# Two scans' loop: which work is given out beside them, and what is queued behind their steps

## The chip, the cores and the metric

One core of a Trainium2 chip runs the whole program. The metric is the time of one execution in microseconds (us), as the device measures it; of the kernel before there are three such times. TensorE (PE) multiplies matrices, VectorE (DVE) and ScalarE (ACT) and GpSimd (POOL) work element by element, and SyncE (SP) issues most of the transfers. Each engine works off its own queue in the order in which the program was laid out.

## The reference

Three layers follow each other. The first is a recurrence over 768 steps for 4 batches with 8 heads of width 40, with a 40 x 40 state for each:

```python
for t in range(S):
    y[:, :, t] = np.einsum('bhd,bhde->bhe', rt, state)
    Sa = np.einsum('bhde,bhe->bhd', state, at)
    state_decay = state * wt[:, :, None, :] - np.einsum('bhd,bhe->bhde', Sa, bt)
    state = state_decay + np.einsum('bhd,bhe->bhde', vt, kt)
# y becomes x: 3072 tokens x 320
h = x @ w_in;  g = np.maximum(h, 0) + alpha * np.minimum(h, 0);  x = g @ w_out      # 320 -> 2048 -> 320
g = x @ w_gate;  out = (g / (1 + np.exp(-g)) * (x @ w_val)) @ w_out                  # 320 -> 1536 -> 320
```

All is float32; the products are made of split operands (a rounded part and its rest), three matmuls for one.

## The kernel before

**Stages.** The 768 steps are cut into 6 blocks m of 128 steps; with 4 batches that makes 24 items, numbered 0 to 23, four for each block. An item goes through `preps` (lines 555 to 638 and 842: decays, scaled operands, small products; all four engines). The four items of one block then share one `inverse(m)` (line 647), the forward substitution that inverts small triangular matrices: VectorE transposes (L650), 31 steps of a product (L665) and a subtraction (L673) on VectorE, each needing the one before, two more transposes (L676, L678), and a tail of tiny matmuls and copies (L686 to L713). Then each item goes through `seq` (line 722), the scan: two chunks of 64 steps, each a strict chain zp (L769), zs (L771, ACT), pp (L779), ut and pv (L781, L783, ACT), transposes (L787, L791), gs and s0 (L793, L798, ACT), gp (L802), a masked product (L805, DVE), yp (L817, L821), the state and the output (L825, L746, L829, DVE and POOL). Two items are scanned side by side. The item's result leaves by a transfer that ScalarE's queue issues (L837). `mlp1(j)` is the first MLP for the tokens of block j, and the second MLP comes last, after all scans.

**Weights.** The inputs' weights are taken apart and rounded into split tiles. For the first MLP, `conv1` makes 32 tiles (two for each of 16 slices f) with two ACT operations (L191, L192), one DVE operation (L193), an ACT copy and a POOL subtraction (L217, L218), and stores them (L264). Twelve of them are made before the first scans. `mlp1` fetches them again (L284).

**The order.** `drive` (line 141) takes several generators with a weight each. At every turn it lets the one that is least far along, by steps done over weight, trace its next step. What is traced earlier gets the higher priority, and a third number lifts a generator's priority; a scheduler then lays each engine's queue out by these priorities and by its own estimate of when operands are ready. The scans and `rest1` have the same lift (`SP` and `HP2`, 3000), the weights' tiles less (`CP`, 2000), `mlp1` none. `rest1` is the chain of what is left of the preparation of items 4 to 7 and `inverse(1)`: 21 steps (one was taken earlier) and 40 steps.

**Ties.** `drive` can also keep the last instruction that each of the first `lead` generators, the scans, has traced on each engine; with `engs` (a bit for each of PE, DVE, ACT, POOL), `lag` and `who`, the other generators' instructions of the same engine must then come behind it in that engine's queue:

```python
if e[4] >= lead and who >> (e[4] - lead) & 1:
    for b in range(4):
        log = crit.get(b, [])
        if engs >> b & 1 and len(log) >= lag:
            st.enter_context(tc.issue_after(log[-lag]))
```

With `engs=0`, the default, nothing is tied. A tie is an order in one queue; it adds no semaphore. Besides, `behind` (line 869) has each tile's DVE instruction come after the last traced step of the substitution.

**Around the change.** Lines 900 to 903 run `inverse(0)` and form `rest1`. Lines 912 to 916 are the loop of scans 0 and 1, here *loop one*; all of `rest1` and 20 tiles go with it. Line 917 gives back the boot pools (two PSUM pools, and buffers of items 0 to 7). Lines 927 to 931 are the loop of scans 2 and 3, *loop two*: nothing of `rest1` is left for it, and 17 steps of `mlp1(0)` go with it. These treat the first 8 slices f for the tokens of batches 0 and 1 alone (256 columns: *half slices*), so that they need only scans 0 and 1; the half slices of batches 2 and 3 and then 8 whole slices follow. `mlp1` has one PSUM buffer for its upper products (line 921). Scans 4 to 7 need `inverse(1)`.

Of the kernel before, what the change touches and what calls it, by code (L numbers as in the profile page):

```python
# [16 lines left out]
FAC = 1.0  # L17
# [28 lines left out]
RA = 1.0  # L46
MP = 0
YB = 1
CP = 2000
HP2 = 3000  # L50
# [23 lines left out]
def kernel(  # L74
# [66 lines left out]
    def drive(*gens, lead=0, engs=0, lag=1, who=0):  # L141
        live = [[*g, 0, j] for j, g in enumerate(gens)]
        names = ["PE", "DVE", "Activation", "Pool"]
        while live:
            e = min(live, key=lambda e: e[3] / e[1])
            try:
                tc.cur_priority -= e[2]
                with ExitStack() as st:
# [5 lines that stand above are left out]
                    n0 = len(traced())  # L154
                    ok = next(e[0], 0)
                    if e[4] < lead:
                        new = traced()[n0:]
                        for b in range(4):
                            mine = [x for x in new if str(x.engine).split(".")[-1] == names[b]]
                            if mine:  # L160
                                crit.setdefault(b, []).append(mine[-1])
                tc.cur_priority += e[2]
                e[3] += 1
                if ok == 0:
                    live.remove(e)
            except StopIteration:
                tc.cur_priority += e[2]
                live.remove(e)

    def chain(*gens):  # L170
        for g in gens:
            yield from g
# [172 lines left out]
    def conv1():  # L345
        for f in range(K1):
            conv(stage, 2 * f, moe_w_in, f, "up")
            yield
            conv(stage, 2 * f + 1, moe_w_out, f, "down")
            yield  # L350

    def conv2():
        for f in range(KEEP):
            for j, (src, kind) in enumerate(((moe2_w_gate, "up"), (moe2_w_val, "up"), (moe2_w_out, "down2"))):
                conv(stage, 2 * K1 + 3 * f + j, src, f, kind)
                yield
# [502 lines left out]
    c1, c2 = conv1(), conv2()  # L859
    NC1, NC2 = 2 * K1, 3 * K2  # L860

    def after(ins, g):
        while True:
            with tc.issue_after(ins.ins):
                if next(g, 0) == 0:
                    return
            yield

    def behind(g):
        while True:  # L870
            with tc.issue_after(mark["inv"].ins) if "inv" in mark else nullcontext():
                if next(g, 0) == 0:
                    return
            yield
# [10 lines left out]
    def take(g, n):  # L885
        for _ in range(n):
            if next(g, 0) == 0:
                return
            yield

    EC0 = 2
    EC = 10
# [5 lines left out]
    c1 = after(mark["prep"], c1)  # L898
    p1, c1 = behind(p1), behind(c1)
    drive((inverse(0), N_INV, HP), (take(p1, EP), EP + .1, BP), (take(c1, EC), EC + .1, CP), lead=1, engs=G0, lag=LG0, who=W0)  # L900
    p1, c1 = after(mark["inv"], p1), after(mark["inv"], c1)
    rest1 = chain(p1, inverse(1))
    nrest = B * N_PREP - EP + N_INV
    if FA == 0:
        drive(
            *((chain(seq(j, j), seq(j + 2, j)), 2 * N_SEQ, SP) for j in range(2)),
            (rest1, FAC * nrest, HP2),
            (take(c1, NC1), NC1 - EC - EC0, CP),
            lead=2, engs=G1, lag=LG1, who=W1,
        )  # L910
    else:
        drive(
            (seq(0, 0), N_SEQ, SP), (seq(1, 1), N_SEQ, SP),
            (take(rest1, int(nrest * RA)) if RA < 1 else rest1, FAC * nrest, HP2),
            (take(c1, NC1), NC1 - EC - EC0, CP),
        )
    boot.close()
    ps1 = ctx.enter_context(ExitStack())
# [7 lines left out]
    if FA:  # L926
        drive(
            (seq(2, 0), N_SEQ, SP), (seq(3, 1), N_SEQ, SP),
            (rest1, FAC * nrest * (1 - RA) + .1, HP2),
            (take(gms[0], 2 * FA + 1), 2 * FA + 1, MP),  # L930
        )
    for m in range(1, NM):
# [201 lines left out]
```

## Time and profile before

| | |
|---|---|
| three runs | 1223.40, 1226.69, 1228.44 us; median 1226.69 us |
| the profiled execution | 1225.27 us, of which its span is 1223.6 us |
| granted TensorE clock, mean of the span | 0.952 |
| PE, DVE, ACT, POOL busy | 1107.1, 735.3, 607.1, 272.0 us |
| loop one's scans (items 0 and 1) | last step 137.3 to 137.7 us |
| `inverse(1)` on VectorE | 120.8 to 185.6 us |
| loop two's scans (items 2 and 3) | last step 178.3 to 178.7 us |

Times in the rows are from the span's start. In a row of the timeline stand the start, the time, the engine (a q behind it: its sequencer, which issues a transfer), the line, the operation, what is written and read, the count, and in brackets the engine's idle time before it with what ended it. A row of the groups gives a line's instructions: count, busy time, mean of one in ns, and idle time before them. A row of the stretches gives its length and then for each engine the busy time and the count, the granted TensorE clock (1.00 is 2.4 GHz), the busy share of the DMA engines and their GB/s.

### The profile page before, as it was taken

What the parts mean: (1) busy time and instruction counts of PE and PEld (TensorE: products, weight loads), DVE (VectorE), ACT (ScalarE), POOL (GpSimd) and SP (SyncE); (2) the same over time, 40 slices, a digit from 0 to 9 for tenths busy, and PEclk for the clock granted to TensorE, in tenths of its full rate; (3) what the DMA queues carried; (4) which work ended last, traced back from release to release, by engine and by line L of the source; (5) the groups of instructions that cost most, each with busy time, mean ns of one, the idle gap of its engine ahead of it and who ended that gap; (6) DMA issues with size and microseconds to landing.
All of it is one profiled execution on the core that took longest, in us unless ns stands there. A gap on an engine that the chain in (4) does not pass through costs nothing. (4 is left out here: it accounts for less than half of the span.)

```text
span 1223.6 us, 24425 instructions
## 1 busy us (share of the span) xinstructions
PE 1107.1 (90%) x9098; PEld 935.2 (76%) x9098; DVE 735.3 (60%) x1592; ACT 607.1 (50%) x1514; POOL 272.0 (22%) x434
## 2 busy tenths in 40 slices
PE   4566678999999989899898999999999999999998
PEld 3345567877878778787686777788788888888887
DVE  7787897698499569859664434879532323223222
ACT  5769658645844764673654433555332323222222
POOL 8115333301212221521363000536300000000000
PEclk9659787999999999899989999999999999999999
DMA  4565697466454544545585473795010101010000
GB/s 145 179 198 176 210 310 228 138 200 185 132 170 137 170 140 148 181 133 147 160 269 189 129 221 135 261 351 158 1 48 1 48 1 48 2 39 9 22 1 21
DMA packets 94884, 166.35 MB, mean 136 GB/s; under 512 B 13232, under 2 KB 43184, under 8 KB 94768
## 3 DMA queue, kind: packets, MB, share of 16 engines
q1 hardware_dynamic: 86608, 160.88, 41.8%
q10 hardware_dynamic: 8160, 3.93, 1.1%
q8 instruction: 72, 1.18, 0.4%
q14 instruction: 44, 0.36, 0.1%
HBM read 136.98 MB, written 27.79 MB: 135 GB/s over the span
## 5 line engine op out<-in xcount | busy, mean ns | idle before, releaser
L217 ACT CAST gh<-g 128x512 fp32r<-128x512 f32 (+1 forms) x176 | 105.5, 600 | 165.0 <-DVE g L1070 115.9
L218 DVE TENSOR_TENSOR gl<-g,gh 128x512 fp32r<-128x512 f32 (+1 forms) x176 | 124.2, 706 | 89.5 <-ACT gh L217 87.1
L1070 DVE TENSOR_TENSOR g<-pv,sg 128x512 f32<-128x512 f32 x72 | 49.8, 691 | 206.3 <-PE pv L294 201.6
L294 PE MATMUL u<-xh,wt 128*128 128x512 f32 (+1 forms) x416 | 147.4, 397 | 11.9 <-DVE g L335 11.0
L335 DVE SCALAR_TENSOR_TENSOR g<-g,neg,u 128x512 f32<-128x512 f32 (+1 forms) x104 | 72.8, 702 | 70.4 <-ACT g L334 69.8
L294 PEld LDWEIGHTS u<-xh,wt 128*128 128x128 f32 x416 | 79.7, 194 | 31.4 <-DVE g L335 14.3
L1068 ACT ACTIVATE sg<-pg 128x512 f32<-128x512 f32 x72 | 43.1, 598 | 121.1 <-PE pg L294 121.1
L294 PE MATMUL pg<-xh,w 128*128 128x512 f32 x288 | 102.5, 394 | 0.0
L294 PE MATMUL pv<-xh,w 128*128 128x512 f32 x288 | 100.4, 389 | 0.0
L334 ACT ACTIVATE g<-u 128x512 f32<-128x512 f32 (+1 forms) x104 | 58.6, 564 | 82.7 <-PE u L294 69.9
L1054 PE MATMUL o<-w,gh 128*128 128x320 f32 x288 | 87.5, 309 | 2.6 <-ACT gh L217 2.6
L1055 PE MATMUL o<-w,gh 128*128 128x320 f32 x288 | 87.8, 309 | 0.0
L301 PE MATMUL d<-gl,wt 128*128 128x512 f32 (+1 forms) x208 | 83.2, 402 | 2.2 <-DVE gl L218 2.2
L604 PE MATMUL mnp<-AN,kbt 128*128 128x128 f32 x384 | 60.1, 307 | 25.6 <-DVE AN L579 13.6
L665 DVE TENSOR_TENSOR tmp<-la 128x96 f32<-128x96 f32 (+43 forms) x306 | 79.5, 286 | 2.7 <-POOL la L653 0.7
L294 PE MATMUL u<-xl,wt 128*128 128x512 f32 (+1 forms) x208 | 80.2, 385 | 0.0
L302 PE MATMUL d<-gh,wt 128*128 128x512 f32 (+1 forms) x208 | 79.9, 386 | 0.0
L1056 PE MATMUL o<-w,gl 128*128 128x320 f32 x288 | 77.2, 310 | 1.0 <-DVE gl L218 0.9
L673 DVE TENSOR_TENSOR la<-la,tmp 128x96 f32<-128x96 f32 (+43 forms) x306 | 76.8, 277 | 2.0
L760 POOL COPY gs<-raw_v 64x160 f32<-64x160 f32 x96 | 43.3, 451 | 148.8 <-PE yp L817 72.2
L618 POOL TENSOR_SCALAR_AFFINE_SELECT AN<-AN 64x256 f32<-64x256 f32 x96 | 50.2, 523 | 117.9 <-ACT AN L617 98.4
L604 PEld LDWEIGHTS mnp<-AN,kbt 128*128 128x128 f32 x384 | 53.4, 214 | 30.0 <-DVE AN L579 13.6
(129 smaller groups left out, 2630.1 us busy)
## 6 DMA issues: line engine op xcount, KB each, us to landing
wt<-wd SPq DMA_DIRECT2D x98, 384.0 KB
wt<-wd SPq DMA_DIRECT2D x98, 320.0 KB
wd<-wc SPq DMA_DIRECT2D x24, 384.0 KB
raw<-in_moe_w_out_dram SPq DMA_DIRECT2D x28, 320.0 KB
raw_bk<-in_bk_dram SPq DMA_DIRECT2D x48, 160.0 KB
wd<-wc SPq DMA_DIRECT2D x20, 320.0 KB
raw<-in_moe_w_in_dram SPq DMA_DIRECT2D x16, 256.0 KB
raw_v<-in_v_dram SPq DMA_DIRECT2D x24, 160.0 KB
```

The costliest lines, as they stand in the source:

```text
L217: nc.scalar.copy(out=h, in_=raw)
L218: eng.tensor_tensor(out=l, in0=raw, in1=h.bitcast(F32), op=ALU.subtract)
L294: last = nc.tensor.matmul(ps, lt, rh, start=(i == 0), stop=(i == len(ops) - 1))
L301: nc.tensor.matmul(ps, wh, gl, start=False, stop=False)
L302: nc.tensor.matmul(ps, wl, gh, start=False, stop=last)
L335: nc.vector.scalar_tensor_tensor(g, g, neg[:, f:f + 1], ps, ALU.mult, ALU.add)
L604: nc.tensor.matmul(ps[:, s].rearrange("p h t -> p (h t)"), kbt[:, g * SH + s].rearrange("p j t -> p (j t)"), an[:, :, g * SH + s, :],)
L665: nc.vector.tensor_tensor(out=tv, in0=ml[:, kk + 1:HALF, kk:kk + 1].to_broadcast([128, nr, ns]), in1=tl[:, kk:kk + 1, c0:c0 + ns].to_broad ...
L673: mark["inv"] = nc.vector.tensor_tensor(out=dst, in0=dst, in1=tv, op=ALU.subtract)
L1054: nc.tensor.matmul(ops[q], gh[:, ts], wh, start=first, stop=False)
L1055: nc.tensor.matmul(ops[q], gh[:, ts], wl, start=False, stop=False)
L1056: nc.tensor.matmul(ops[q], gl[:, ts], wh, start=False, stop=last)
```

## The change

Loop one takes 27 steps of `rest1` and 9 tiles, with weights 27 and 9; since `rest1` has 21 steps of preparation left, the last 6 of the 27 are the first of `inverse(1)` (its first transposition and 5 of the 31 steps). It also ties both: `lead=2` (the two scans), `engs=6` (DVE and ACT), `lag=1` (the newest step), `who=3` (both other generators). Loop two gets the other 34 steps of `rest1`, weight 40, and the other 11 tiles, weight 11, without ties. Nothing is computed in another way.

```diff
     else:
         drive(
             (seq(0, 0), N_SEQ, SP), (seq(1, 1), N_SEQ, SP),
-            (take(rest1, int(nrest * RA)) if RA < 1 else rest1, FAC * nrest, HP2),
-            (take(c1, NC1), NC1 - EC - EC0, CP),
+            (take(rest1, 27), 27, HP2),
+            (take(c1, 9), 9, CP),
+            lead=2, engs=6, lag=1, who=3,
         )
@@
     if FA:
         drive(
             (seq(2, 0), N_SEQ, SP), (seq(3, 1), N_SEQ, SP),
-            (rest1, FAC * nrest * (1 - RA) + .1, HP2),
+            (rest1, nrest - 27, HP2),
+            (take(c1, NC1), NC1 - EC - EC0 - 9, CP),
             (take(gms[0], 2 * FA + 1), 2 * FA + 1, MP),
         )
```

Here `nrest` is 67, `N_SEQ` 13, `NC1` 32, `EC` 10, `EC0` 2, `FA` 8.

## Rows read from the trace of the kernel before

**Rows 1.** The page's busy times of the engines, of the whole span

```profile
PE 1107.1 (90%) x9098; PEld 935.2 (76%) x9098; DVE 735.3 (60%) x1592; ACT 607.1 (50%) x1514; POOL 272.0 (22%) x434
```

**Rows 2.** Stretches: length, then PE, PEld, DVE, ACT, POOL, clock, DMA

```profile
95.00:137.00 42.00, 28.88 (x373) 25.10 (x373) 31.01 (x63) 34.32 (x108) 23.15 (x38) 0.88 0.55 174
137.00:200.00 63.00, 46.38 (x671) 41.27 (x672) 57.36 (x152) 41.51 (x117) 21.66 (x34) 0.77 0.85 278
200.00:700.00 500.00, 467.54 (x5090) 392.18 (x5091) 359.51 (x893) 298.57 (x818) 133.58 (x242) 0.97 0.54 165
...
137.00:183.00 46.00, 34.77 (x376) 30.46 (x376) 43.17 (x132) 27.78 (x87) 16.25 (x27) 0.81 0.86 285
183.00:200.00 17.00, 11.61 (x295) 10.80 (x296) 14.19 (x21) 13.73 (x31) 5.40 (x7) 0.65 0.81 260
...
800.00:1000.00 200.00, 196.38 (x983) 168.74 (x983) 98.47 (x148) 73.29 (x134) 38.26 (x33) 1.00 0.26 85
```

**Rows 3.** ScalarE's groups by line, 95 to 137 us

```profile
L617 ACT COPY AN<-mnp 64x256 f32<-64x256 f32 x12 | 4.4, 367 | 0.2
L610 ACT COPY tt<-mnp 64x256 f32<-64x256 f32 x12 | 4.4, 366 | 0.1
L217 ACT CAST wc<-wz 128x256 fp32r<-128x256 f32 (+2 forms) x12 | 4.3, 391 | 1.6 <-DVE wz L193 0.9 <-DMA wd<-wc 0.7
L191 ACT ACTIVATE wz<-raw 128x384 f32<-128x384 f32 (+1 forms) x8 | 4.2, 528 | 1.2 <-DMA raw<-in_moe_w_out_dram 1.2
L192 ACT ACTIVATE wy<-raw 128x384 uint32<-128x384 uint16 (+1 forms) x7 | 3.7, 528 | 0.0
```

**Rows 4.** Timeline, scans 0 and 1: where ScalarE's copies stand behind TensorE

```profile
95.88 1.15 PE L779 MATMUL pp<-tt,zs 128*64 128x64 f32 x30
...
103.89 0.37 ACT L781 COPY ut<-pp 128x256 f32<-128x256 f32 x1
...
106.83 0.38 PE L791 MATMUL pp<-ident,ST 128*128 128x128 f32 x2
...
110.96 0.61 ACT L793 ACTIVATE gs<-pp 64x160 f32<-64x160 f32 x2
...
119.97 0.98 PE L769 MATMUL zp<-gs,AN 128*64 128x40 f32 x16 [0.77 <-DVE gs L746]
...
122.79 1.18 ACT L771 COPY zs<-zp 64x160 f32<-64x160 f32 x4
...
135.86 0.59 ACT L771 COPY zs<-zp 64x160 f32<-64x160 f32 x2 [3.33 <-PE zp L769]
```

**Rows 5.** VectorE: groups 120 to 138 us, then the substitution's ends (timeline)

```profile
L665 DVE TENSOR_TENSOR tmp<-la 128x31 f32<-128x31 f32 (+11 forms) x12 | 3.8, 348 | 0.3 <-POOL la L653 0.3
L673 DVE TENSOR_TENSOR la<-la,tmp 128x31 f32<-128x31 f32 (+9 forms) x10 | 3.3, 354 | 0.1
...
L650 DVE STREAM_TRANSPOSE la<-tt 128x1024 f32<-128x1024 f32 x1 | 2.0, 1970 | 0.6 <-ACT tt L613 0.6
...
120.79 1.97 DVE L650 STREAM_TRANSPOSE la<-tt 128x1024 f32<-128x1024 f32 x1 [0.62 <-ACT tt L613]
...
183.66 1.91 DVE L678 STREAM_TRANSPOSE tt<-la 128x1024 f32<-128x1024 f32 x1
```

**Rows 6.** Timeline: from the end of scans 0 and 1 to what follows

```profile
137.27 0.41 DVE L829 TENSOR_TENSOR pv<-yp,Wx 128x256 f32<-128x256 f32 x1
...
141.76 0.71 ACT L737 COPY pv<-raw_vt 128x256 f32<-128x256 f32 x2 [3.87 <-DMA raw<-in_moe_w_out_dram]
...
145.18 0.82 SPq L319 DMA_DIRECT2D xa<-xd  x2
...
149.73 0.36 PE L294 MATMUL u<-xh,wt 128*128 128x256 f32 x1
```

**Rows 7.** TensorE's timeline: the first half slices of `mlp1(0)`

```profile
161.62 0.58 PE L294 MATMUL u<-xh,wt 128*128 128x256 f32 x1
...
165.45 0.48 PE L300 MATMUL d<-gh,wt 128*128 128x256 f32 x2
...
167.20 0.40 PE L294 MATMUL u<-xst,wt 128*128 128x256 f32 x2
...
180.53 0.28 PE L294 MATMUL u<-xh,wt 128*128 128x256 f32 x1
```

## The prediction

> **What bounds the kernel now.** I read the busy times of the whole span first. TensorE is busy 1107.1 of 1223.6 us, so 116.5 us are idle in all; VectorE (735.3) and ScalarE (607.1) are far from the span [rows 1]. Next I cut the span into stretches [rows 2]. From 800 us on TensorE is busy 196.4 of 200 us at full clock: that end can't be moved. From 200 to 700 us it is busy 467.5 of 500 us, with VectorE at 72%: TensorE is the limit there too, and work that it has not done by 200 us is simply appended. From 95 to 200 us it is another kernel: 75.3 of 105 us, granted clock 0.88 and then 0.77. There the limit is first ScalarE (34.3 of 42 us up to 137 us) and then VectorE (57.4 of 63 us, and 43.2 of 46 up to 183 us). The change touches nothing outside this stretch, so its value is read there and nowhere else: **how much earlier does TensorE reach the state that it has at 200 us, and how much more has it done by then?** Two numbers carry the answer. L is by how much scans 0 and 1 end earlier than 137 us; S is by how much the substitution's end on VectorE (185.6 us, with the tail that follows it) moves, positive for later.
>
> **Loop one: the ties (L).** ScalarE's timeline shows the cost that they aim at [rows 4]. The pp products of both scans end at 97.0 us, and the first ut copy that reads them starts at 103.9: 6.9 us. The transposes end at 107.2, the gs copies start at 111.0: 3.8 us. The second zp ends at 120.9, the zs copies start at 122.8: 1.8 us. In these 12.5 us ScalarE worked on fillers that had been traced earlier. They were earlier because `rest1` has weight 67: it makes 5.2 steps for each step of a scan, so all 21 steps of preparation are traced by the scans' fifth step of 13. With weight 27 it makes 2.1, and the tie puts each batch behind the newest scan step. So 12.5 us is the upper bound of L. The lower one for a ScalarE that never waits: its 34.3 busy us of this loop, begun at 95 us, end at 129.3 us, which is L = 7.7. If the weights' tiles slip behind the scans (12.2 us of ScalarE's groups, the last three of [rows 3]; they have the lower priority, but 9 of them are still given out here), L grows toward the upper bound. I take **L = 8**, near the lower bound, because the preparation that leaves the first chunk only moves into the second, where ScalarE had room. What the ties can cost below that is the third rival.
>
> What is queued behind the tied instructions: on ScalarE the copies of the preparation (8.8 us in its two largest groups [rows 3]) and the tiles' copies; on VectorE the decays and products of items 5 to 7 and L193; and at the end whatever ScalarE has after the issue of the scans' output transfers (L837), which counts as a step of a scan. Behind those wait GpSimd's selections and subtractions, SP's stores (L264) and the loads that refill the raw buffers. None of these is asked for before the substitution (the copies of item 7) or the later slices (the tiles), so I cost them at nothing as long as the preparation ends with the scans; SP and GpSimd have room (GpSimd 23.2 of 42 us [rows 2]).
>
> **Loop one: the substitution leaves (part of S).** Now it starts at 120.8 us [rows 5], under the second chunk of scans 0 and 1, and has 3.8 + 3.3 + 2.0 = 9.1 us done by 138 us. After the change six steps of it are still traced in loop one, behind nearly all of the scans; I count 3 of the 9.1 us there (the transposition, 2.0 us, and five small steps) and 6.1 us as moved to loop two. The preparation ends some 4 to 8 us later than now, since it is strung along the scans.
>
> **Loop two (S).** VectorE had 43.2 busy us in the 46 us from 137 to 183 [rows 2], a share of 0.94. After the change the same stretch starts L = 8 us earlier, at 129, and holds 6.1 us more: 49.3 / 0.94 = 52.5 us, which ends at 181.5. So **S = -1.5 us**. Within loop two the substitution no longer outranks scans 2 and 3, since both are now traced in turn; that changes who goes first, but both have to be through by the end of this stretch in either kernel (scans 2 and 3 end at 178 us now), so the sum holds. The 11 tiles stay chained to the substitution's steps by `behind`, as now; their VectorE and ScalarE time is in the same stretch before and after, and I cost their move at nothing. If it were not covered, they would be late for the ninth slice, which TensorE reaches only after 16 half slices.
>
> **What TensorE gains.** The scans' result has to reach memory and come back: from the last step at 137.3 us to the new scans' first copy at 141.8, to the load of x at 145.2 and the first upper product at 149.7 [rows 6]. All four hang on scans 0 and 1 and move by L. (The pools that line 917 gives back hang on item 7's preparation; if it ends by 129 us, it is ready long before 145 - 8 = 137.) From there the half slices go one in 4.7 us (161.6 to 180.5 in four) [rows 7], because one PSUM buffer goes round TensorE, ScalarE and VectorE; one of them is 2.15 us of TensorE (165.45 to 167.60). Between their start and the end of the substitution there are now L + S = 8 - 1.5 = 6.5 us more: 6.5 / 4.7 x 2.15 = 3.0 us of work done beforehand. The state of 200 us itself comes 1.5 us earlier. Sum: **1.5 + 3.0 = 4.5 us gained**, and in general gain = -S + (L + S) x 0.46. The tail from 183 to 200 us, where TensorE is busy 11.6 of 17 us at clock 0.65 [rows 2], stays as it is in this sum. What is late next is that tail: the substitution's transposes, tiny matmuls and copies.
>
> The profiled execution took 1225.27 us, 1.4 under the median of the three runs; 1225.3 - 4.5 = 1220.8, and at the median **1226.7 - 4.5 = 1222.2 us**.
>
> **Trace and notes.** The granted clock fell to 0.65 in the tail and was 0.88 in loop one [rows 2]; a mean between the levels of 1.2 and 2.4 GHz (0.5 and 1.0) says that the engine changed between them. If half slices fill idle places there, part of the work would also run at the higher level. I leave that out of the sum and put it into the first rival.
>
> One rule speaks against this change. The Trainium skill, "Perfetto Trace Analysis", section "Optimization Strategy", says that where the most-contended engine changes over time, interleaving the regimes may help. The kernel before does that: VectorE's substitution under ScalarE's preparation. By that rule taking it apart gives the gain back; the second rival prices this from rows, and no row of before tells which wins.
>
> **The rivals.** First, *the whole lead is kept*. L is the full 12.5 us, and VectorE, freed of queues that wait, gets the substitution done as early as the scans: S = -8. Gain 8 + 4.5 x 0.46 = 10.1 us: 1216.6. For it: the idle 30 us of TensorE from 95 to 200 us and the low clock leave the room. Against it: VectorE at 0.94 in the second part [rows 2].
>
> Second, *given back*: L = 8, but the substitution loses its whole cover of 9.1 us, S = +9.1, since it comes second in loop two and its chain of dependent steps finds no other idle place. Gain -9.1 + 17.1 x 0.46 = -1.2 us: 1227.9, no change. The same answer would come if the change did nothing to the order, because the preparation is ScalarE's bound either way.
>
> Third, *the ties make engines wait*, and it is slower. ScalarE works in order; with everything tied behind the newest step, a copy that waits for TensorE holds the fillers up as well. When the scans' copies had no filler before them, they waited up to 3.33 us (135.9 us [rows 4]). There are 8 such stops in two chunks; at some 1.5 us each (my estimate, between nothing and 3.33) that is 12 us, against 7.7 us for which ScalarE is idle in this loop now. Then the scans end 4 us late, L = -4, and the substitution, still without cover, S = 4 + 9.1 = 13.1: gain -13.1 + 9.1 x 0.46 = -8.9 us, 1235.6. It decides from the point where ScalarE's idle time in loop one passes those 7.7 us. For it: TensorE's steps are slow there, at clock 0.88. Against it: each batch of two steps of preparation and most of a tile, some 3 us, is about as long as TensorE's part between two stops.
>
> **How the numbers follow.** The forecast gets 0.45, the whole lead 0.21, given back 0.14, slower 0.20. The forecast's own range is 4 us to either side, 1218.2 to 1226.2. The range for 8 in 10 goes from 1213 (most of the first rival) to 1234 (a part of the third); the rest of the third rival and the far end of the first lie outside. A measurement of this kernel can tell about 0.5%, 6.1 us, from no change: faster means under 1220.6. Of the forecast's 0.45 I put 0.20 below that and 0.25 within; the first rival is all faster; the second all the same; of the third 0.18 are slower and 0.02 the same. Faster 0.41, same 0.41, slower 0.18.
>
> **What would show it.** Right: ut copies within 2 us of the pp products, scans 0 and 1 at their last step at 125 to 132 us, L650 at 124 to 130, the first half slice's product near 141, L678 ending between 180 and 188, and TensorE full from about 195 us, with the later part unchanged. Wrong: ScalarE idle for more than 8 us between 95 and the end of the scans (third rival); L678 past 190 (second); L678 before 180 with the scans at 125 (first). If scans 2 and 3 or the transfers around 130 to 170 us take longer than now, the term of 3.0 us goes. And if anything after 250 us differs by more than a few us, the argument that the rest is only appended is wrong.

## The result, and the profile after

The changed kernel takes 1233.49 us (median of 7 runs, 1229.81 to 1235.4), the kernel before in the same runs 1226.69 (7 runs, 1222.11 to 1229.2): a ratio of 1.0055, 95% interval 1.0037 to 1.0072. It is 6.8 us slower, where 4.5 us faster was forecast; 1222.2 was predicted, and 1233.5 lies at the upper end of the range for 8 in 10 (1213 to 1234). The profiled execution has a span of 1233.5 us at a mean granted clock of 0.944 (before: 1223.6 and 0.952).

The page's busy times of the whole span, which answer to [rows 1]:

```profile
PE 1108.8 (90%) x9098; PEld 941.1 (76%) x9098; DVE 738.9 (60%) x1592; ACT 606.9 (49%) x1514; POOL 268.7 (22%) x434
```

The work is the same. Of the 9.9 us by which the span is longer, TensorE's busy time has 1.7 us and its idle time 8.2. The stretches, as in [rows 2] (length, then PE, PEld, DVE, ACT, POOL, clock, DMA):

```profile
95.00:137.00 42.00, 28.79 (x406) 25.93 (x403) 34.28 (x56) 34.34 (x107) 22.62 (x36) 0.87 0.46 151
137.00:200.00 63.00, 44.42 (x604) 40.22 (x605) 58.25 (x162) 41.52 (x113) 23.08 (x37) 0.72 0.83 268
200.00:700.00 500.00, 462.85 (x5011) 390.63 (x5010) 360.25 (x890) 291.67 (x802) 130.36 (x242) 0.95 0.53 165
137.00:183.00 46.00, 30.52 (x320) 26.87 (x320) 42.75 (x142) 28.61 (x86) 16.54 (x30) 0.79 0.82 267
183.00:200.00 17.00, 13.90 (x284) 13.35 (x285) 15.50 (x21) 12.90 (x28) 6.54 (x7) 0.52 0.85 273
800.00:1000.00 200.00, 196.35 (x974) 167.94 (x973) 102.61 (x153) 74.45 (x137) 43.13 (x38) 1.00 0.29 98
```

Two things are to be seen. From 137 to 183 us TensorE does 4.3 us less than before (30.5 for 34.8), though the scans got there earlier. And from 200 to 700 us, in loops whose code is untouched, it does 4.7 us less (462.9 for 467.5), at a clock of 0.95 for 0.97. Only the end from 800 us on is as it was.

The timeline of the first 200 us, which answers to [rows 4], [rows 5] and [rows 6]: the scans' copies, their last step, the new scans, x, the first half slice, and the substitution's ends.

```profile
94.81 1.15 PE L779 MATMUL pp<-tt,zs 128*64 128x64 f32 x32
95.54 0.37 ACT L781 COPY ut<-pp 128x256 f32<-128x256 f32 x1 [0.81 <-PE pp L779]
...
98.79 0.62 ACT L793 ACTIVATE gs<-pp 64x160 f32<-64x160 f32 x2
...
129.82 0.41 DVE L829 TENSOR_TENSOR pv<-yp,Wx 128x256 f32<-128x256 f32 x1
130.15 1.93 DVE L650 STREAM_TRANSPOSE la<-tt 128x1024 f32<-128x1024 f32 x1
...
134.25 0.71 ACT L737 COPY pv<-raw_vt 128x256 f32<-128x256 f32 x2 [3.46 <-DMA raw<-in_moe_w_in_dram]
...
141.37 0.94 SPq L319 DMA_DIRECT2D xa<-xd  x2
...
154.73 2.03 SPq L284 DMA_DIRECT2D wt<-wd  x4
...
160.30 0.58 PE L294 MATMUL u<-xh,wt 128*128 128x256 f32 x1
...
161.75 0.63 PE L294 MATMUL u<-xst,wt 128*128 128x256 f32 x2
...
184.10 1.93 DVE L678 STREAM_TRANSPOSE tt<-la 128x1024 f32<-128x1024 f32 x1
```

The ut copy now follows its products at once (95.54 for 103.89), the last scan step ends at 130.2 for 137.7, and the substitution begins behind it (130.15) and ends where it did (its last transposition starts at 184.10 for 183.66). But the first upper product of `mlp1(0)` starts at 160.30 instead of 149.73. In the kernel before, 149.73 is only the first of its eight matmuls; the last two, which need the last part of x, come nine us later:

```profile
158.68 0.80 PE L294 MATMUL u<-xst,wt 128*128 128x256 f32 x2
```

Measured by its end the first upper product is late by 2.9 us (162.4 for 159.5): the lead of the scans has turned into a delay on its way.

**A measure for the whole program.** From each trace I took, for every time, how many columns TensorE's matmuls had moved by then. The *lag* of a kernel at a time is how much later it has done what the kernel before had done at that time. For the changed kernel it is -6.1 us at 137 (ahead), +1.1 at 160, +8.9 at 183, +3.6 at 200, +6.1 at 300, +15.7 at 400, +15.0 at 660 and +9.9 from 800 us to the end. The lag rests on one execution of each kernel: two traces of one and the same program (n28 and n28r below) differ by 0.6 us at 200 and by 7.2 at 900. These two executions took 1232.55 and 1225.41 us, and a traced execution isn't always near the median (fetchup's took 1252.8, its median is 1243.5). Where a stop falls on the time asked for, the lag jumps by its length. So only the timed runs decide what a kernel costs, and lags of some us late in the program are no evidence alone.

### The profile page after: what moved, and what is told of

Same layout as the page of the kernel before. It is cut to its first block, busy times and chain, and to the rows that moved or that the text cites. A ratio compares the mean times of both kernels' runs of the same rounds, so it can differ in the third digit from the quotient of the medians.

```text
span 1233.5 us, 24442 instructions
## 1 busy us (share of the span) xinstructions
PE 1108.8 (90%) x9098; PEld 941.1 (76%) x9098; DVE 738.9 (60%) x1592; ACT 606.9 (49%) x1514; POOL 268.7 (22%) x434
## 3 DMA queue, kind: packets, MB, share of 16 engines
q10 hardware_dynamic: 8160, 3.93, 1.1%
## 4 chain that ended last, share of the span: by engine, by line
PE 57%; DVE 16%; DMA 9%; ACT 9%; issue 4%; POOL 2%; SPq 1%; ACTq 0%; DVEq 0%; POOLq 0%
PE pg L294 10%; PE u L294 9%; PE pv L294 9%; PE o L1058 3%; PE o L1057 3%; PE o L1056 3%; PE d L301 2%; PE d L300 2%; PE d L302 2%; PE mnp L604 2%; PE gp L802 2%; DMA xd<-pv 2%; DVE la L673 2%; DVE tmp L665 2%; PE yp L817 2%
## 5 line engine op out<-in xcount | busy, mean ns | idle before, releaser
L218 DVE TENSOR_TENSOR gl<-g,gh 128x512 fp32r<-128x512 f32 (+1 forms) x176 | 122.5, 696 | 89.7 <-ACT gh L217 87.6
L294 PE MATMUL u<-xh,wt 128*128 128x512 f32 (+1 forms) x416 | 147.3, 397 | 7.9 <-DVE g L335 4.5
L294 PE MATMUL pg<-xh,w 128*128 128x512 f32 x288 | 102.5, 394 | 0.0
L294 PEld LDWEIGHTS u<-xh,wt 128*128 128x128 f32 x416 | 79.9, 195 | 27.2 <-DVE g L335 9.3
L294 PE MATMUL pv<-xh,w 128*128 128x512 f32 x288 | 100.5, 389 | 0.0
L294 PE MATMUL u<-xl,wt 128*128 128x512 f32 (+1 forms) x208 | 80.3, 386 | 0.0
L665 DVE TENSOR_TENSOR tmp<-la 128x96 f32<-128x96 f32 (+43 forms) x306 | 76.4, 275 | 2.8 <-POOL la L653 0.9
```

The costliest lines, as they stand in the source:

```text
L218: eng.tensor_tensor(out=l, in0=raw, in1=h.bitcast(F32), op=ALU.subtract)
L294: last = nc.tensor.matmul(ps, lt, rh, start=(i == 0), stop=(i == len(ops) - 1))
L665: nc.vector.tensor_tensor(out=tv, in0=ml[:, kk + 1:HALF, kk:kk + 1].to_broadcast([128, nr, ns]), in1=tl[:, kk:kk + 1, c0:c0 + ns].to_broad ...
```

## The experiments

Ratios are to the kernel before, in runs on the same chip, with the 95% interval; its medians there were 1228.5 to 1230.7 us (1226.7 for the first row). A kernel has 4 to 12 timed runs, the kernel before 7 to 29. The last column counts the TensorE instructions of the loops m = 1 to 5 and of what follows (5768) that stand at another place among themselves than in the kernel before.

| kernel | ratio | lag at 160, 200, 300, 900 us | moved |
|---|---|---|---|
| changed kernel | 1.0055 [1.0037, 1.0072] | 1.1, 3.6, 6.1, 9.9 | 2487 |
| ties | 1.0132 [1.0087, 1.0178] | 9.8, 14.2, 16.0, 19.6 | 3196 |
| shares | 1.0021 [0.9998, 1.0045] | 4.2, 8.1, 5.2, 8.6 | 2835 |
| fetchup | 1.0138 [1.0092, 1.0185] | -3.1, 12.8, 21.1, 27.6 | 3132 |
| fetchlate | 1.0111 [1.0064, 1.0158] | 2.6, 2.6, 12.8, 11.2 | 2858 |
| frz | 1.0084 [1.0061, 1.0107] | 0.7, 3.8, 11.5, 11.1 | 0 |
| rfrz | 1.0051 [1.0028, 1.0074] | 1.0, 0.6, 9.0, 9.8 | 2487 |
| up2 | 1.0087 [1.0061, 1.0112] | 5.8, 7.5, 10.9, 10.7 | 2487 |
| frzup | 1.0099 [1.0060, 1.0138] | 5.4, 8.6, 14.0, 16.6 | 0 |
| frzld | 1.0090 [1.0059, 1.0121] | -0.6, 8.0, 9.4, 11.1 | 0 |
| pv_after | 1.0167 [1.0128, 1.0206] | 3.2, 12.4, 18.1, 27.1 | 2487 |
| pv_before | 1.0180 [1.0145, 1.0216] | 2.6, 2.7, 8.9, 30.3 | 0 |
| n26 | 1.0129 [1.0088, 1.0169] | 0.6, 14.3, 24.0, 26.9 | 2678 |
| n28 | 0.9972 [0.9953, 0.9991] | 3.4, 3.1, 2.3, 7.0 | 2780 |
| n28r, the same again | 0.9970 [0.9949, 0.9990] | 3.9, 3.7, 2.5, -0.2 | 2780 |
| t10 | 0.9971 [0.9950, 0.9992] | 1.0, 10.4, 9.8, 3.7 | 2490 |
| t10r, the same again | 0.9996 [0.9977, 1.0015] | 0.7, 10.5, 9.7, 6.3 | 2490 |
| t11 | 0.9998 [0.9977, 1.0020] | 0.4, -2.2, -3.0, 2.0 | 3086 |
| n28t11 | 1.0025 [1.0009, 1.0041] | 2.9, 7.8, 8.8, 8.9 | 1048 |

### The two halves of the change, and the fetches

*ties* is the kernel before with nothing but the ties; *shares* is the changed kernel without them:

```diff
 # ties: kernel before
             (take(c1, NC1), NC1 - EC - EC0, CP),
+            lead=2, engs=6, lag=1, who=3,
 # shares: changed kernel
             (take(c1, 9), 9, CP),
-            lead=2, engs=6, lag=1, who=3,
```

> The kernel before with the ties of loop one alone; all of rest1 and 20 tiles stay in loop one. Theory A (late fetch: the loss is that the first MLP's first weight fetches stand some 19 us later in SyncE's queue, behind loads and stores of tiles, 154.7 against 135.7 us): decided by where the fetches come to stand, here 5 places later than before, so near the kernel before, within 4 us of 1226. Theory B (lost cover: the substitution no longer runs under the first two scans): here it is given out as before, so no slower than before, 1220 to 1227. Theory C (the ties themselves cost, engines wait in order): slower by about 6, 1231 to 1235.

> The changed kernel without the ties: 27 steps and 9 tiles in loop one, the rest in loop two. Theory A: the fetches stand as late as in the changed kernel, so 1230 to 1236. Theory B: the substitution has lost its cover, 1231 to 1236 as well. Theory C: without the ties no loss, 1224 to 1228. A and B are told apart by the first upper product of the half slices (A: at 158 us or later, with the substitution's end under 186 us; B: the substitution's end past 190 us).

Ties alone cost 1.3%, 15 us, more than any of the theories had (theory C: about 6): scans 0 and 1 end at 149.9 us, 12 later than before, and from 95 us to there ScalarE is idle for 14.8 us (7.7 in the kernel before to its scans' end, 4.2 in the changed one). That is the prediction's third rival by its own sign, ScalarE idle for over 8 us, in the kernel that has the ties without the new weights. The shares alone cost 0.2%, not clear of no change, with the scans' end at 141.6. Together the two cost 0.55%: their effects don't add (1.3 + 0.2), and the scans' lead comes only with both.

*fetchup* gives the first four weight fetches of `mlp1(0)` a higher priority in the changed kernel; *fetchlate* puts those of the kernel before behind its loads of x:

```diff
 # fetchup
-        with held_by(ago(AHEAD)) if idx in resident else nullcontext():
+        with held_by(ago(AHEAD)) if idx in resident else lifted(2500) if j == 0 and len(fetched) < 4 else nullcontext():
 # fetchlate; mark["xa"] is the last load of x (L323)
+        with held_by(ago(AHEAD)) if idx in resident else tc.issue_after(mark["xa"].ins) if j == 0 and len(fetched) < 4 else nullcontext():
```

> The changed kernel with the first four weight fetches of the first MLP lifted by 2500, so that they stand 26 places earlier in SyncE's queue; nothing else is edited. Theory A: the first upper product comes at 142 to 150 us and not at 160.3, and at 200 us TensorE is no longer behind the kernel before; time 1224 to 1229. Theory B and C: the fetch was not what held it, 1231 to 1236.

> The kernel before with the first four weight fetches of the first MLP put behind the loads of x in SyncE's queue (15 places later); nothing else is edited. Theory A: the first upper product moves from 149.7 to about 158 us and the time grows by 3 to 6 us, 1229 to 1233. Theories B and C: within 2 us of before.

fetchup brings the start of the first upper product back to 150.9 us (its end to 158.1), with the scans' lead kept (end at 131.3), and yet the kernel is 1.4% slower than before; of its lag of 27.6 us, 12.8 stand by 200 us already. fetchlate loses 2.6 us by 200 us (3 to 6 were expected in all) and then another 10 between 240 and 300 us, where nothing of the edit is left. So a small edit in the first 160 us changes something far behind it. The orders of the queues say what: the scheduler lays out each queue of the whole program by priorities and by its own estimate of times, and of the 5768 TensorE instructions behind loop two 2487 stand elsewhere in the changed kernel than before (613 of 1182 of ScalarE, 698 of 1238 of VectorE, 241 of 561 transfers of SP), though not a line of theirs was changed. This became theory D: the new order of the untouched loops costs the time.

### Holding the order

To separate the first 200 us from the later order, I wrote an order out in the kernel: the numbers of the instructions traced from loop m = 1 on, engine by engine, as they stand in the other kernel, each tied behind the one before it in its queue (an order only, no semaphore):

```diff
+    for o in ORDER:                       # one list for each engine
+        for p, q in zip(o, o[1:]):
+            tc.add_manual_dep(al[cut + q], al[cut + p].name, NO_SYNC, reason="order")
```

*frz* has the changed first part and the later order of before; *rfrz* has the first part of before and the later order of the changed kernel. Holding costs nothing by itself: with its own later order written out in this way, either kernel is built as the same program as without, instruction for instruction and wait for wait on every engine (12793 in the changed kernel, 12776 in the kernel before).

> The changed kernel, but everything that is traced in the loops m = 1 to 5 and behind them stands on each engine in the order that the kernel before gives it (5768 instructions of TensorE, 1238 of VectorE, 1182 of ScalarE, 300 of GpSimd, 561 transfers of SP); what is traced before these loops stands as in the changed kernel. Nothing is left out. Theory D (the scheduler gives the later loops, whose code is unchanged, another order, and that order is what costs): TensorE is as late at 200 us as in the changed kernel, 3.6 us, and no later at the end: 1226.7 + 3.6, some 1230 us (1228 to 1232). Theory A (the lateness of the first fetches and of the first half slices costs it all, and the later order doesn't matter): as the changed kernel, 1233.5 us (1232 to 1236).

> The reverse: the kernel before, but what is traced in the loops m = 1 to 5 and behind them stands in the order that the changed kernel has. Theory D: the first 200 us are as before, and the end is later by what the changed kernel loses from 200 us on, 9.9 - 3.6 = 6.3 us: 1233 us (1230 to 1236). Theory A: as before, 1227 us (1225 to 1229).

rfrz is as slow as the changed kernel (1.0051 for 1.0055), as theory D expected, although its first part is that of before (143 of TensorE's 822 instructions there, among them the half slices, stand a little differently) and TensorE is only 0.6 us late at 200 us. **The later order alone is enough for the whole loss.** What the order brings with it is seen in TensorE's timeline: the stops of over 2 us between 200 and 500 us, first of the changed kernel, then the same of rfrz (its lines are numbered 292 higher; it has one more, of 2.14 us at 298.4). Before has none of that length in this stretch.

```profile
249.56 1.98 PE L779 MATMUL pp<-tt,zs 128*64 128x64 f32 x32 [3.45 <-ACT zs L771]
...
359.18 1.97 PE L779 MATMUL pp<-tt,zs 128*64 128x64 f32 x32 [4.25 <-ACT zs L771]
...
414.15 1.12 PE L632 MATMUL kbp<-ident,kbt 128*128 128x128 f32 x4 [4.06 <-ACT AN L617]
...
467.56 1.12 PE L779 MATMUL pp<-tt,zs 128*64 128x64 f32 x16 [2.39 <-ACT zs L771]
```

```profile
250.33 1.98 PE L1071 MATMUL pp<-tt,zs 128*64 128x64 f32 x32 [3.20 <-ACT zs L1063]
...
361.19 1.73 PE L1071 MATMUL pp<-tt,zs 128*64 128x64 f32 x32 [4.03 <-ACT zs L1063]
...
416.10 1.07 PE L924 MATMUL kbp<-ident,kbt 128*128 128x128 f32 x4 [4.89 <-ACT AN L909]
...
468.68 0.69 PE L1071 MATMUL pp<-tt,zs 128*64 128x64 f32 x16 [2.34 <-ACT zs L1063]
```

A fifth, 6.95 and 6.96 us behind AN, stands at 526.4 and 526.8 us. The same stops in two kernels with different first parts belong to the order. What they cost can't be read off by adding them up: the five have 21.1 us, while the lag grows by 6.3 us from 200 us to the end; the kernel before has stops of its own elsewhere (the longest 4.08 us at 612.6). Nor is it idle time alone: of the 9.7 us by which the span of rfrz is longer than that of before, 8.3 are busy time of TensorE (1115.4 for 1107.1) at a mean granted clock of 0.941 for 0.952. ScalarE's timeline at the first of them, in the changed kernel and then, around the same scans, in the kernel before:

```profile
243.08 2.40 ACTq L837 DMA_DIRECT2D xd<-pv  x4
248.31 0.71 ACT L737 COPY pv<-raw_vt 128x256 f32<-128x256 f32 x2 [7.67 <-DMA xd<-pv]
248.93 1.19 ACT L771 COPY zs<-zp 64x160 f32<-64x160 f32 x4
```

```profile
236.77 0.70 ACTq L837 DMA_DIRECT2D xd<-pv  x2
...
239.23 0.58 ACT L771 COPY zs<-zp 64x160 f32<-64x160 f32 x2
240.13 0.71 ACT L737 COPY pv<-raw_vt 128x256 f32<-128x256 f32 x2 [0.32 <-DMA xd<-pv]
...
241.64 0.76 ACTq L837 DMA_DIRECT2D xd<-pv  x2
242.45 0.58 ACT L771 COPY zs<-zp 64x160 f32<-64x160 f32 x2 [1.20 <-PE zp L769]
```

Before, the two scans' output transfers go out 5 us apart, and the zs copy stands ahead of the copy of raw_vt that waits for the output transfer. In the changed order both scans run in step. ScalarE is idle for 7.67 us: 2.4 until the first of four transfers goes out, 2.4 while they are issued one behind the other, and 2.8 until the copy (L737) may start; all four zs copies stand behind it. Their zp products had started at 244.53 and 245.44 us and take 0.7 us each. The Trainium skill, "TensorE: Matmul & The Clock Gate", section "Architectural detail: the array is 16× 32×32, not 1× 128×128", states that ScalarE and VectorE take their instructions strictly in order; this trace agrees, with copies ready by some 246.2 us that start at 248.93.

frz, however, isn't better but worse (1.0084, where 1230 us, 1.003, was expected): with the old later order the changed first part is 3.8 us late at 200 us, as it was, and then stops once more. TensorE, ScalarE and SP's queue in frz (lines 292 higher; L1079 is L787, L852 is L560, L556 is L264, L576 is L284, L804 and L803 are L512 and L511):

```profile
213.67 0.69 PE L1079 MATMUL pp<-ident,ut 128*128 128x128 f32 x2 [5.26 <-ACT pv L1075]
```

```profile
211.21 0.62 ACT L852 COPY wseg<-raw_w 128x512 f32<-128x512 f32 x1 [2.58 <-DMA raw_w<-in_wa_dram]
```

```profile
194.43 5.13 SPq L556 DMA_DIRECT2D wd<-wc  x2
199.65 5.74 SPq L576 DMA_DIRECT2D wt<-wd  x3
...
206.49 0.84 SPq L804 DMA_DIRECT2D raw_a<-in_wa_dram  x2
207.38 0.70 SPq L803 DMA_DIRECT2D raw_w<-in_wa_dram  x2
```

In these rows SP works through its transfers in order too. A store that waits for GpSimd and three fetches that wait for TensorE hold it from 194.4 to 205.4 us; the load of raw_w stands behind them, ScalarE's copy waits for the load, the scan's pv copies stand behind that copy, and TensorE waits 5.26 us. From 210 us on the lag of frz stays near that (10.3 at 210, 12.1 at 600, 11.1 at the end): what isn't done by then is appended, as the prediction said, but only while the later order is held.

### Taking single waits away

With the order held, single instructions can be moved and nothing else. Each time the kernel is the changed one, frz (in frzup and frzld) or the kernel before (in pv_before), with every order held, and only the list of one engine is edited:

```diff
 # up2, frzup (SP): the four fetches of fetchup, two ahead of the loads of x, two behind their last part
-... xa(719) xa(716) ... xa(713) ... xa(712) ... wt(705) wt(615) wt(575) wt(545)
+... wt(705) wt(615) ... xa(719) xa(716) ... xa(713) ... xa(712) wt(575) wt(545) ...
 # frzld (SP): two loads of raw_a and two of raw_w, ahead of the store and the three fetches
-raw_bk wd(171) wt(86) raw raw wd(87) wd(14) wt(31) wt(13) wt raw raw raw_a raw_a raw_w raw_w
+raw_bk raw_a raw_a raw_w raw_w wd(171) wt(86) raw raw wd(87) wd(14) wt(31) wt(13) wt raw raw
 # pv_after, pv_before (ACT): L737 of a scan in the loops m = 1 to 5
-L737 L737 L771 L771 ... L781 L783 L783
+L771 L771 ... L781 L783 L783 L737 L737
```

> The changed kernel with every engine's order held as it is there, but for SP: the first four fetches of weights stand where the kernel before has them, two ahead of the loads of x and two behind their last part, and no longer behind the tiles' loads and stores. Theory A: the first upper product starts near 151 us instead of 160.3 and the end comes 8 to 11 us earlier, 1222.5 to 1225.5 us. Theory D: the first product is as early, TensorE gains up to 10 us by 170 us, but the later order is still the changed one: by 200 us it keeps 3 to 5 us, and the end lies between 1228 and 1233 us.

> Both: the changed kernel's first part with the first four fetches of weights at the place of before, and the later loops in the order of before. Theory D with A's local part: frz less 3 to 8 us, 1220 to 1227 us, at or under the kernel before, and the lead of 7.4 us of scans 0 and 1 is to be seen in TensorE's work at 160 us. If it isn't below 1227 us, the local loss has another cause than the fetches (substitution's cover, the tiles in loop two).

> The kernel with the changed first part and the later loops in the order of before (frz), every order held, and on SP alone four transfers moved: the loads of raw_a and raw_w that land at 210 us stand ahead of the store of a weight tile (waited for until 199.7) and the three fetches (until 205.4) that they stood behind. Theory G (a load behind transfers that wait in SP's in-order queue makes ScalarE and VectorE wait, and behind their copies the scans, and so TensorE): TensorE's stop of 5.26 us at 213.7 us goes or falls under 1.5 us, and the kernel is 4 to 6 us faster than frz, a ratio to the kernel before of 1.003 to 1.006. Rival (another transfer is as late): the stop only changes its place, ratio 1.007 to 1.010 as frz.

> The changed kernel with every engine's order held, but for ScalarE in the loops m = 1 to 5: the first copies of a scan (L737, pv from raw_vt), which wait for a transfer, stand behind the same scan's first zs, ut and pv copies, or 8 places further down where that is over 18 places away. Theory E (in ScalarE's in-order queue these copies wait for the output transfer of the scan before, or for the load of raw_vt, and the scans' zs copies and the preparation's AN copies, for which TensorE waits, stand behind them): of TensorE's five stops at 249.6, 359.2, 414.2, 467.6 and 526.4 us (3.45, 4.25, 4.06, 2.39 and 6.95, 21.1 us in all) at least two thirds go, and the end comes 5 to 12 us earlier than the changed kernel's 1233.5: 1221 to 1228 us. Rival F (the wait only moves to the products that read pv, gp): 1231 to 1236 us.

> The same edit in the kernel before. Its stops of TensorE behind zs between 200 and 700 us are 3.6 us longer than 1 us each (1.88 and 1.71). Theory E: little to gain, 1222 to 1227 us. Rival F: 1227 to 1235 us, slower, since the copies are put off without need.

None of them gained anything, and of the expectations only that of frzld's rival held. Where the wait went is seen in the traces.

*up2, frzup.* The first two fetches go out at 140 and 141 us and the next two at 152 (in frzup a us earlier), and the first product still starts at 165 us in both. It was not the fetch alone for which it waited. In up2 (lines 351 higher; L542 is L191, L1122 is L771, L1130 is L779, L645 is L294) ScalarE and TensorE show:

```profile
161.18 0.55 ACT L542 ACTIVATE wz<-raw 128x384 f32<-128x384 f32 x1 [4.95 <-DMA raw<-in_moe_w_in_dram]
161.62 0.57 ACT L1122 COPY zs<-zp 64x160 f32<-64x160 f32 x2
```

```profile
162.24 1.12 PE L1130 MATMUL pp<-tt,zs 128*64 128x64 f32 x16 [2.65 <-ACT zs L1122]
...
164.94 0.58 PE L645 MATMUL u<-xh,wt 128*128 128x256 f32 x1
```

A tile's first ScalarE operation waits 4.95 us for its raw load; the zs copy of scans 2 and 3 stands behind it, their pp product behind the zs, and the half slice behind pp in TensorE's queue. In the changed kernel itself the same row reads 2.93 us, and the half slice follows pp as closely (there the fetches go out at 154.73 and could hold it too):

```profile
156.54 0.55 ACT L191 ACTIVATE wz<-raw 128x384 f32<-128x384 f32 x1 [2.93 <-DMA raw<-in_moe_w_in_dram]
156.99 0.57 ACT L771 COPY zs<-zp 64x160 f32<-64x160 f32 x2
```

```profile
159.25 1.12 PE L779 MATMUL pp<-tt,zs 128*64 128x64 f32 x16 [0.52 <-ACT zs L771]
160.30 0.58 PE L294 MATMUL u<-xh,wt 128*128 128x256 f32 x1
```

That is the smaller part of the lost lead. Followed along the first of scans 2 and 3, the lead over the kernel before is 5.2 us at its yp product (144.86 for 150.02), 2.1 at the next zp (152.59 for 154.66) and nothing at its zs (156.99 for 157.01). The first 3.1 us go on VectorE. TensorE's stop there, in the changed kernel and then in the kernel before:

```profile
152.59 1.44 PE L769 MATMUL zp<-gs,AN 128*64 128x40 f32 x18 [4.48 <-DVE gs L746]
```

```profile
154.66 0.99 PE L769 MATMUL zp<-gs,AN 128*64 128x40 f32 x16 [1.17 <-DVE gs L746]
```

The state (L825) that gs needs stands 3.3 us behind the yp product in the changed kernel, 1.2 before. In VectorE's queue the other scan's masked product, steps of the substitution, a tile's L193, which waits for ScalarE, and the split of x (L218) come first:

```profile
147.92 0.49 DVE L193 SCALAR_TENSOR_TENSOR wz<-wz,wy 128x320 uint32<-128x320 uint32 x1 [0.76 <-ACT wy L192]
...
149.49 0.32 DVE L825 TENSOR_TENSOR ST<-yp,ST 128x160 f32<-128x160 f32 x1
```

In up2 such an L193 waits 3.77 us (147.69), a masked product stands behind it, and TensorE stops for 5.00 us (148.91). From 137 to 183 us the tiles' first operation (L191) waits 6.9 us for raw loads in the changed kernel and 1.2 in the kernel before, L193 4.0 us for ScalarE and 0.9. How much of the delay is the tiles' and how much the substitution's, no run separates.

*frzld.* The stop at 213.7 us shrinks to 2.78 us (at 215.3), and a new one of 3.93 us stands at 202.6: the weight store now goes out later, and ScalarE's next tile copy, which writes the stored buffer, waits 5.65 us for it. The rival's answer holds, 1.0090.

*pv_after, pv_before.* Of the five stops those at 250 and 359 us fall to 1.4 us each, those behind AN stay (6.10 and 5.24), and the kernel loses 9 us more at once, between 183 and 200 us. SP's queue, ScalarE and TensorE in pv_after (L615 is L264, L898 is the load of raw_vt, L547, L670 that of x, L635 the fetch; L1088 is L737, L651 is L300):

```profile
182.78 0.38 SPq L615 DMA_DIRECT2D wd<-wc  x1
192.12 0.68 SPq L898 DMA_DIRECT2D raw_vt<-in_vt_dram  x2
192.89 0.82 SPq L670 DMA_DIRECT2D xa<-xd  x2
...
194.99 1.96 SPq L635 DMA_DIRECT2D wt<-wd  x4
```

```profile
191.38 0.71 ACT L1088 COPY pv<-raw_vt 128x256 f32<-128x256 f32 x2
```

```profile
198.54 0.58 PE L651 MATMUL d<-gh,wt 128*128 128x256 f32 x1 [8.20 <-DMA wt<-wd]
```

The copy that was put off frees the buffer of raw_vt only at 192.1 us; the next load of raw_vt waits for that at the head of SP's queue from 183.2 on, the loads of x and the fetches of weights stand behind it, and TensorE waits 8.20 us for them. In pv_before 1254.7 us came where 1222 to 1235 was expected; its lag is 8.9 us at 300 and 30.3 at 900 us, and from 200 to 760 us TensorE waits 17.2 us for fetches of weights (2.0 in the kernel before), the longest 6.89 at 646 us. Theory E named a true wait and a wrong remedy; rival F looked for the wait in gp and missed its place as well.

### The neighbours

What one step more or less in loop one does, with nothing held:

```diff
-            (take(rest1, 27), 27, HP2),      # n26, n28: 26, 28
-            (take(c1, 9), 9, CP),            # t10, t11: 10, 11; n28t11: 28 and 11
```

> The changed kernel with 26 instead of 27 steps of preparation and substitution in loop one; nothing is held. The step moved is one small step of the substitution. Theory D (any edit in the first 200 us makes the scheduler order the later loops anew, for better or worse): anything from 1222 to 1245 us, with other stops of TensorE in other places. Rival (the time follows the edit): within 1.5 us of the changed kernel, 1232 to 1235 us.

> The changed kernel with 10 instead of 9 tiles in loop one; nothing is held. Theory D: anything from 1222 to 1245 us, and not the same as with 26 steps. Rival: within 1.5 us of the changed kernel, 1232 to 1235 us.

> The changed kernel with 11 instead of 9 tiles in loop one; nothing is held. Theory D (one step more or less gives the whole program another order, for better or worse): a ratio to the kernel before between 0.997 and 1.015, no nearer to that of ten tiles (0.9971) than to that of nine (1.0055). Rival (more tiles in loop one are better): 0.990 to 0.998.

> The changed kernel with 28 instead of 27 steps of preparation and substitution in loop one; nothing is held. Theory D: between 0.997 and 1.015. Rival (the time follows the count of steps: 26 gave 1.0129, 27 gave 1.0055): 0.996 to 1.001.

> Ten tiles in loop one once more, on another chip run. If it is faster than the kernel before and not by the chance of the runs: a ratio of 0.994 to 0.999 again. Otherwise 1.000 to 1.003.

> 28 steps once more, on another chip run: if the gain isn't by the chance of the runs, a ratio to the kernel before of 0.995 to 0.999 again; otherwise 1.000 to 1.002.

> 28 steps and 11 tiles in loop one together. If each step moved had a price of its own, the two gains over the changed kernel add (1.0055 to 0.9972 and to 0.9998, some 8 and 6 points of a thousand): a ratio of 0.990 to 0.993. Theory D (each edit is a new order, and the gains don't add): 0.996 to 1.012.

One small step of 40 moves the time from 1.0129 over 1.0055 to 0.9972, and one tile from 1.0055 to about 0.998 (the middle of the two runs of t10). n26 is 0.4 us ahead at 150 us, but what before had done by 183 us it has done 22 us later, at 205: most of its loss is local, and in it TensorE waits 7.32 us for a fetch (190.3 to 197.7 us). t10 is 10 us late at 200 and makes most of that good later. Its gain was not confirmed: t10r gave 0.9996, between the two answers that were named. Three counts of steps in a falling row could be a trend, but 28 steps and 11 tiles together give 1.0025, where prices of their own would have given 1.0055 - 0.0083 - 0.0057 = 0.9915; and this kernel has the later order that is nearest to that of before (1048 moved) and is slower than n28 with 2780. Theory D holds in this: an edit of this size is a new order of the whole program, and its time is spread over at least 0.997 to 1.013. How much of that lies in the later loops was not held apart for these kernels. t11's expectation missed in a point: it lies nearer to ten tiles than to nine.

**n28 is the fastest kernel seen**: 0.9972 and 0.9970 in two chip runs, by these ratios some 3.5 us under the kernel before and 10 under the changed one. The granted clock, as the mean of the timed runs, is 0.952 in n28 and n28r, 0.948 to 0.950 in the kernel before beside them, and 0.944 in the changed kernel and in rfrz. Whether an order costs by its stops or by the clock that goes with them, no run separates.

## Why the prediction was wrong

*L, the scans of loop one: right.* L = 8 was taken, and 137.7 - 130.2 = 7.5 us came. ScalarE waits 0.81 us for the first pp products and copies ut at once, and from 95 us to the scans' end it is idle for 4.2 us where it was 7.7, so the ties made it wait no longer; in this kernel the third rival didn't come about.

*The substitution: right to 2 us.* It begins at 130.15 us (124 to 130 was named) and S is +0.4 us instead of -1.5. VectorE's share from 137 to 183 us is 0.93, as in the sum. The second rival put the loss of the interleaving at 9.1 us; no row shows that. The Trainium skill, "Perfetto Trace Analysis", section "Optimization Strategy", which the prediction weighed, says that interleaving such regimes may help; no run here shows what that is worth.

*The half slices: the first step that failed.* "All four hang on scans 0 and 1 and move by L" is wrong. The new scans' copy moved by 7.5 us (134.25) and the first load of x by 3.8; the first product starts 10.6 us later and ends 2.9 later. The prediction had taken its first matmul (149.73) for the product, which in the kernel before was through only at 159.5. The sum of loop two gave the moved tiles no cost but late slices ("their VectorE and ScalarE time is in the same stretch"). That is the term that was put at nothing. Their price wasn't busy time but place in two queues: a tile's first ScalarE operation waits for its raw load with the scan's zs behind it (2.93 us at 156.5), and on VectorE the scan's state stands behind a tile's L193 and steps of the substitution, where TensorE stops for 4.48 us instead of 1.17. So the first of scans 2 and 3 lost its lead of 5.2 us by its second zs (157.0 as before), the other kept 2.5 (158.6 for 161.1), and the half slice stands behind them on TensorE. The waits are in the rows; that the tiles alone cause them is argued, since no run moved the tiles and nothing else with the order held. What should have been 3.0 us of work beforehand became 4.3 us of TensorE less up to 183 us. The prediction had listed SP among the queues that the tiles pass, and counted the engines' room instead of their order. Instead of 4.5 us ahead, TensorE is 3.6 us late at 200 us.

*"Simply appended": the second step that failed.* The prediction named its own test: if anything after 250 us differs by more than a few us, this argument is wrong. It does. rfrz shows that the later order by itself costs as much as the whole change (1.0051), frz that without it the first part costs no less (1.0084): the two losses don't add. That each order is fitted to its own first part, and that the changed kernel's order gives back part of the one loss and adds stops of its own, is my reading and not shown. With the order held, the argument of appending holds (frz). That "the change touches nothing outside this stretch" was true of the code and not of the program.

*The rivals.* "The ties make engines wait" gave 1235.6 us, near the 1233.5 that came, by a mechanism that isn't the one here; that it came so near is luck. It is luck, too, that 1233.5 still lies within the range for 8 in 10, which reached that far only for this rival. None of the rivals had the order of untouched loops in it; a spread of about 0.8% for it to either side, as the neighbours show, would have been the honest width.

What stays open: why one order is better than another, and how much of its price is stops and how much clock. The runs name single waits (L737 behind the output transfers, raw loads behind stores and fetches), but each attempt to take one away in a held order made another queue wait, so none of them is shown to be worth what it shows. A version in which the scans' output transfers and loads go by a queue of their own wasn't tried.

## What to carry to other kernels

Where a scheduler lays out the queues, an edit changes the order of the whole program, so compare the instruction order of the code that wasn't touched, and time a few neighbours of the edit (one step more, one less) before a difference of 1% is put down to it. Holding the order in one part shows which part it comes from. In these kernels a transfer or copy that waited at the head of a queue held what stood behind it, and moving it moved the wait to another queue each time: count the queue's order, not its busy share. A lead on the critical chain is worth what the next shared queue lets through. And read where a product ends, not only where its first matmul starts.

## What the runs showed of the hardware

Two executions of one program, with one order (n28, n28r), took 1232.55 and 1225.41 us, while the medians of their runs agree (1225.45 and 1225.22 us). Of the 7.1 us between them 6.7 are busy time of TensorE (1115.1 and 1108.4 us for the same 9098 matmuls) at a mean granted clock of 0.947 and 0.954, between the levels of 1.2 and 2.4 GHz: the difference is hardly idle time. And four output transfers issued together by ScalarE's queue (2.40 us) kept the copy behind them until 2.8 us after the last was issued, 5.2 us of the 7.67 in which ScalarE did nothing.
